# Two first-layer outputs of a fused attention and feed-forward kernel share three cycles of eight stream slots, and their f16 parts move from DVE to POOL

## The chip, the cores and the metric

The kernel runs on one core of one Trainium2 chip. The metric is the device time of one execution in microseconds. Inside the core, PE multiplies matrices, ACT (ScalarE) evaluates exponentials and tanh, DVE (VectorE) does elementwise work, POOL (GpSimd) can do elementwise work on data in SBUF and issues some DMAs, and SP issues most DMAs.

## The reference

The kernel computes a gated sum of an attention with one shared key and value head (32 query heads of width 16) and a feed-forward layer, both of the same `x` (2048 tokens of width 512; the hidden width is 1792):

```
q = (x @ wq) as 32 heads of 16;  k = x @ wk;  v = x @ wv
a = softmax(q k^T / 4) v, heads joined, @ wo
b = silu(x @ w1) @ w2
g = sigmoid(sum(x * gate_w))
out = g * a + (1 - g) * b
```

Everything is f32 at the borders. Inside, the kernel writes an f32 operand as the sum of two f16 parts and multiplies three products of parts (high by high, high by low, low by high).

## The kernel before, in words

A short prologue transposes `x` into f16 parts, makes the keys, values and gate, and the first query blocks. Then `attention` runs one long loop, written out by hand in order: each engine takes its instructions in the order in which this loop issues them.

**Steps and cycles.** The attention is cut into 32 rounds (4 query chunks of 512 tokens, 4 groups of heads, 2 halves) of 16 key tiles, so 512 steps. One pass of the main loop, called a cycle here, issues two steps, so there are 256 cycles. A cycle is spelled as a string of slots:

- S is one score slot: 8 small matmuls (L997) into a PSUM tile of two banks, followed by one exponential on ACT (L1000, 128x1024) into `P`. A cycle has four. There are two such PSUM tiles, so PE can be at most two score slots ahead of ACT.
- F is one slot of the *stream* (L741): 4 matmuls for the lower half of the contraction of a new output and 4 for the upper half of the current one, which use different rows of the array. The stream holds everything that isn't attention: the first feed-forward layer (`ffn_h`), the second (`ffn_o`), the query blocks and the output projection. An output is two turns of 12 slots long (fewer for some): first as the new one, then as the current one. When its second turn is over it is evicted from its PSUM bank; there are two such banks (`pm`), so the next new output starts in the bank that has just been evicted.
- P and N multiply probabilities by values (L1043). The odd step of a cycle always does it with one pass of f32 matmuls (N). The even step does it in one of two ways. *Split*: three passes (PPP) of 16-bit matmuls, by the upper 16 bits of `P`, and by the rest `L`, which DVE must have made with two subtractions of 128x1024 (L1021). *Native*: one more f32 pass (N), with no work on DVE.
- B is the place where a bound for a later round may be made.

**What DVE is given.** `spend`, `put` and `fill` keep an account of DVE's time: each known piece of work has a price, each cycle has a length (3.7 us, 4.1 us after a first-layer output), and small jobs (weight parts, range checks) are filled into what is left. `backlog` is what the account is over.

**First-layer outputs.** 56 of them, in 16 blocks of 4, 4, 4 and 2 per query chunk. `evict` does a tanh on ACT (L789, PSUM to `e`), one combination on DVE (L790, `e` and PSUM to `e`, after which the bank is free), and, up to two cycles later, the two f16 parts on DVE (`split_v`: a cast at L120 and a subtraction at L121, `e` to `H`). The second layer reads `H` a block later. There are two `e` buffers.

**Which even steps are split.** `split_step` says native where the current output is a first-layer one and is in the last half of its turn, or where the cycle is a wide one. 174 even steps are split and 82 are native.

**Wide cycles.** Query blocks are extra work in the stream; each adds 12 to a `debt` (18 at the start). A cycle that follows the eviction of a first-layer output has 12 F slots instead of 6 while the debt is 6 or more (`WIDE`). There are 27 of these.

**The end.** After the last step, the rest of the stream runs as plain 128-row matmuls (L745), with the transposes and division of the last round on DVE ahead of the last output projections.

Of the kernel before, what the change touches and what calls it, by code (L numbers as in the profile page):

```python
# [13 lines left out]
OP = mybir.AluOpType  # L14
# [10 lines left out]


SPLIT, NATIVE = "SFFFSFFFSPPPSBN", "SFFFSFFFSNBSN"
WIDE = {SPLIT: "SFFFFFFSFFFFFFSPPPBSN", NATIVE: "SFFFFFFSFFFFFFSNBSN"}

FIRST = "EEEEEEEEEESEESEEEESEEEESBEEEE"  # L30
AHEAD, EARLY = 2, (4, 5)
# [14 lines left out]
def kernel(  # L46
# [21 lines left out]
    nc = tc.nc  # L68
    _, S, D = x.shape
    F = w1.shape[1]  # L70
    DH = wk.shape[1]
    KD = D // 128
# [17 lines left out]
    xs = consts.tile([128, 2, KD, S], F16)  # L90
# [28 lines left out]
    def split_v(a1, a2, a):  # L119
        nc.vector.tensor_copy(a1, a)  # L120
        nc.vector.tensor_tensor(a2, a, a1, op=OP.subtract)  # L121
# [579 lines left out]
    def attention(ctx, scale_of, t_scale, shifts, split_pieces, chores, q_todo, bounds, early, gates_):  # L701
# [46 lines left out]
        backlog, spent, todo, cycle = [0.0], [0.0], [], [0]  # L748

        def spend(t):  # L750
            spent[0] += t

        def put(t, age, f):

            todo.append((t, cycle[0] + age, f))

        def fill(length):
            room = length - backlog[0] - spent[0]
            cycle[0] += 1
            backlog[0], spent[0] = max(0.0, -room), 0.0  # L760
            if bounds and turn[0] and turn[1] == 6 and not turn[0].hidden and not turn[0].is_q:
                return
            while todo and (todo[0][0] <= room or cycle[0] >= todo[0][1]):
                t, _, f = todo.pop(0)
                f()
                room -= t
            if split_pieces.left() and (room >= 1.3 or split_pieces.count < 5.6 + 0.57 * cycle[0]):
                split_pieces.step()
                room -= 1.3
            elif not split_pieces.left() and chores and (room >= 1.1 or cycle[0] > 200):  # L770
                if chores[0]:
                    chores[0].pop(0)()
                    room -= 1.1
                elif not open_q:
                    chores.pop(1)()
                    room -= 1.1
                    if len(chores) == 1:
                        chores.clear()
            backlog[0] = max(0.0, -room)

        def ffn_h(k, f):
            c, g = blocks[k]
            f0 = (sum(GF[:g]) + f) * 128
            cs = slice(c * 512, c * 512 + 512)

            def evict(ph):

                e = wp.tile([128, 512], F32, name="e", bufs=2)
                nc.scalar.activation(e, ph, AF.Tanh, scale=t_scale)  # L789
                nc.vector.scalar_tensor_tensor(e, e, 1.0, ph, op0=OP.add, op1=OP.mult)  # L790
                H = Hs[k, f] = wp.tile([128, 2, 512], F16, name="H", bufs=2 * NF)
                spend(0.62)
                put(1.0, 2, lambda: split_v(H[:, 0], H[:, 1], e))

            assert split_pieces.ready(w1, g), (k, len(split_pieces.done))
            return Out([(lambda i, b, m, n=32, kt=kt: w1s[b, i, kt, f0 + m:f0 + m + n],
                         lambda j, b, kt=kt: xs[b, j, kt, cs]) for kt in range(KD)], evict, hidden=True)

        def ffn_o(k, t):
            c, g = blocks[k]  # L800
# [57 lines left out]
        urgent = []  # L858

        def outs():  # L860

            for k in range(len(blocks) + 1):
                if k < len(blocks):
                    for f in range(GF[blocks[k][1]]):
                        yield ffn_h(k, f)
                        while urgent:
                            yield urgent.pop(0)()
                else:
                    for _ in range(2):
                        yield urgent.pop(0)() if urgent else None  # L870
                if k:
                    for t in range(4):
                        if queue:
                            debt[0] += 12
                            yield q_block(queue.pop(0))
                        yield ffn_o(k - 1, t)
                        while urgent:
                            yield urgent.pop(0)()
            while True:
                yield urgent.pop(0)() if urgent else None  # L880

        def follow():
            if ahead:
                return ahead.pop()
            o = next(seq)
            if o is not None:
                o.bank = pM.tile([128, 512], F32, name="pm")
            return o

        seq, ahead, ended, debt = outs(), [], [None], [18]  # L890
        drains = [0]
        turn = [None, 0]
        lo, hi_ = slice(0, 64), slice(64, 128)
        plain, ending = [False], [False]
# [1 line left out]
        def stream():  # L896

            cur = None
            while True:
                if plain[0] and cur is None:  # L900
                    o = follow()
                    if o is None:
                        return
                    for n in range(len(o.mm)):
                        o.whole(n, n == 0, n == len(o.mm) - 1)
                    o.evict(o.bank)
                    yield True
                    continue
                new = None if plain[0] else follow()
                n_new = len(new.mm) if new else 0  # L910
                n_cur = len(cur.mm) if cur else 0
                n = -(-max(n_new, n_cur) // 6) * 6


                if cur and drains[0] == cur.count and ending[0]:
                    drain()
                for i in range(n):
                    turn[:] = cur, n - i - 1
                    for m in range(4):
                        if i < n_new:  # L920
                            new.product(i, lo, m, i == 0, False)
                        if i < n_cur:
                            cur.product(i, hi_, m, False, i == n_cur - 1)
                    if i < n - 1:
                        yield False
                if cur:
                    cur.evict(cur.bank)
                    ended[0] = cur
                cur = new
                if cur:  # L930
                    cur.count = drains[0]
                yield True

        def drain():

            nc.tensor.drain()
            drains[0] += 1
# [29 lines left out]
        steps = [(i, kt) for i in range(len(rounds)) for kt in range(NKT)]  # L967
# [37 lines left out]

        def split_step(s):

            return steps[s][1] > 0 and not (turn[0] and turn[0].hidden and (0 < turn[1] <= 6 or wide[0]))

        def low(p, s, j):  # L1010

# [48 lines left out]
                split_pieces.step()  # L1060
                yield

        qtile, wide = {}, [False]
        whole_ = early_products()
        work = stream()
        prefetch(0)
        for s in range(0, len(steps) + 2, 2):
            on = s < len(steps)
            ending[0] = not on
            if on and steps[s][1] == 0:  # L1070
                i = steps[s][0]
                prefetch(i + 1)
                if q_todo and i % 2 == 0:
                    queue.append(q_todo.pop(0))
            p, more = 2 * s, True
            slots, order = SPLIT, [(s - 2, 0), (s - 2, 1), (s - 2, 2), (s - 1, 3)]
            if s - 2 in native:
                slots, order = NATIVE, [(s - 2, 3), (s - 1, 3)]
            if not s and early:
                slots = FIRST  # L1080
            wide[0] = debt[0] >= 6 and ended[0] is not None and ended[0].hidden
            if wide[0]:
                slots = WIDE[slots]
            ended[0], n_f, bounded[0] = None, 0, False
            for a in slots:
                if a == "S" and on:
                    scores(p)
                    p += 1
                elif a == "E":
                    next(whole_, None)  # L1090
                elif a == "F" and more:
                    more = not next(work)
                    n_f += 1
                elif a == "B" and (bound_now() or not s and bounds):
                    bound()
                    bounded[0] = True
                    while lq and lq[0][0] <= p - 3:
                        low(*lq.pop(0))
                elif a in "PN" and s >= 2:
                    pv(*order.pop(0))  # L1100
            debt[0] -= max(n_f - 6, 0)
            if gates_ and s == 4:
                gates_()
                spend(0.6)
            fill(4.95 if n_f > 6 else 4.1 if ended[0] and ended[0].hidden else 3.7)
        plain[0] = True
        while todo:
            todo.pop(0)[2]()
# [6 lines left out]
    over = nc.values_load(flag[0:1, 0:1], min_val=0, max_val=1)  # L1115
# [29 lines left out]
```

## Time and profile before

| | |
|---|---|
| three runs | 1078.17, 1079.02, 1079.59 us; median 1079.02 |
| span of the profiled execution | 1075.3 us, 3.7 us under the median; its time outside the span isn't recorded |
| PE busy | 1057.2 us, 98% |
| ACT busy | 1008.6 us, 94% |
| DVE busy | 789.9 us, 73% |
| POOL busy | 23.4 us, 2% |
| main loop, first to last exponential | 39.3 to 1054.2 us of the span |

The page's first part gives busy time, share of the span and number of instructions for each engine. A group row gives line, engine, operation, what is written from what, count, then busy time, mean duration of one, and the idle time of the engine just before. A row of the table of windows gives the stretch, its length and then the busy time of each engine in it with the number of its instructions. A row of the timeline gives start, length, and how many like instructions were merged. Eight matmuls on different parts of the array run together, so the duration of one (375 ns) is not what a slot costs; what a slot costs is the distance from its start to the next slot's.

### The profile page before, as it was taken

How to read it: one execution, taken by the hardware profiler on the slowest of the kernel's cores; microseconds unless marked ns; L12 is line 12 of the kernel's file. 1: busy time of each engine (PE TensorE's matmuls, PEld its weight loads, DVE VectorE, ACT ScalarE, POOL GpSimd, SP SyncE). 2: the span in 40 equal slices, each digit the busy share in tenths (PEclk: the TensorE clock that was granted, in tenths of full speed). 3: DMA queues.
4: the chain of work that ended last, by engine and by line, in shares of the span. 5: the costliest groups of instructions: out<-in, count | busy, mean ns of one | idle time of the engine just before them, and what ended most of it. 6: DMA issues, size and time to landing. Idle time of an engine off the chain costs nothing.

```text
span 1075.3 us, 65967 instructions
## 1 busy us (share of the span) xinstructions
PE 1057.2 (98%) x31224; PEld 667.5 (62%) x31224; DVE 789.9 (73%) x1082; ACT 1008.6 (94%) x1121; POOL 23.4 (2%) x53
## 2 busy tenths in 40 slices
PE   8999999999999999999999999999999999999996
PEld 5455776766665577677655568677756555555552
DVE  6856986968778786878777697675857767476875
ACT  5799999999999999999999999899989999999992
POOL 2110000000000000000000000000000000000000
PEclk9999999999999999999999999999999999999999
DMA  5311111220001000000000100000000110000001
GB/s 208 115 61 45 49 42 31 61 60 14 11 11 41 32 22 10 17 12 12 22 11 21 37 19 21 22 12 11 20 6 12 31 31 12 11 11 5 11 4 43
DMA packets 20840, 32.95 MB, mean 31 GB/s; under 512 B 5137, under 2 KB 12050, under 8 KB 20562
## 3 DMA queue, kind: packets, MB, share of 16 engines
q1 hardware_dynamic: 17618, 20.46, 5.9%
q0 software_dynamic: 2512, 8.13, 2.6%
q8 instruction: 246, 4.03, 1.5%
q14 instruction: 32, 0.26, 0.1%
q10 hardware_dynamic: 432, 0.07, 0.0%
HBM read 20.12 MB, written 8.52 MB: 27 GB/s over the span
## 4 chain that ended last, share of the span: by engine, by line
PE 89%; DVE 5%; ACT 4%; issue 1%; POOL 0%; POOLq 0%; ACTq 0%
PE pv L1043 35%; PE pm L741 31%; PE S L997 19%; ACT P L1000 4%; DVE L L1021 1%; PE pm L745 1%; PE pt L311 0%; PE pk L126 0%; DVE xs L117 0%; DVE T L943 0%; PE pk L127 0%; PE pk L125 0%; DVE U L944 0%; PE pm L342 0%; DVE T L945 0%
## 5 line engine op out<-in xcount | busy, mean ns | idle before, releaser
L1000 ACT ACTIVATE P<-S 128x1024 f32<-128x1024 f32 x1024 | 963.5, 1051 | 24.6 <-PE S L997 19.4
L997 PE MATMUL S<-qb,KT 50*32 50x512 f16 x8192 | 480.1, 378 | 2.3 <-ACT P L1000 2.2
L1021 DVE TENSOR_TENSOR L<-P 128x1024 f16<-128x1024 f32 x348 | 408.1, 1217 | 8.3 <-ACT P L1000 8.2
L1043 PE MATMUL pv<-P,VF 64*32 64x512 f32 x5408 | 374.8, 589 | 0.0
L997 PEld LDWEIGHTS <-KT 50*32 50x32 f16 x8192 | 188.6, 90 | 193.9 <-issue 126.7
L741 PE MATMUL pm<-w2s,H 64*32 64x512 f16 x5232 | 258.8, 375 | 0.6 <-DVE qx L825 0.2
L741 PE MATMUL pm<-xs,w1s 64*32 64x512 f16 x5376 | 248.5, 375 | 1.1 <-issue 0.6
L741 PEld LDWEIGHTS <-H 64*32 64x32 f16 x5232 | 143.7, 93 | 43.5 <-issue 11.3
L741 PEld LDWEIGHTS <-w1s 64*32 64x32 f16 x5376 | 136.3, 93 | 46.1 <-issue 13.5
L1043 PEld LDWEIGHTS pv<-P,VF 64*32 64x32 f32 x5408 | 125.0, 107 | 30.3 <-issue 8.1
L790 DVE SCALAR_TENSOR_TENSOR e<-e,pm 128x512 f32<-128x512 f32 x56 | 38.5, 687 | 140.3 <-ACT e L789 139.4
L1043 PE MATMUL pv<-P,VH 64*32 64x512 bf16 x1392 | 81.9, 389 | 0.0
L1043 PE MATMUL pv<-L,VH 64*32 64x512 f16 x1392 | 81.4, 374 | 0.0
L1043 PE MATMUL pv<-P,VL 64*32 64x512 bf16 x1392 | 81.4, 385 | 0.0
L741 PE MATMUL pm<-xs,wqs 64*32 64x512 f16 x1152 | 81.1, 375 | 0.0
L1043 PEld LDWEIGHTS <-VH 64*32 64x32 f16 x2784 | 60.7, 92 | 20.4 <-issue 3.8
L741 PE MATMUL pm<-wo_s,O 64*32 64x512 f16 x1440 | 63.3, 375 | 0.0
L943 DVE STREAM_TRANSPOSE T<-pv 128x512 f32<-128x512 f32 x32 | 23.0, 717 | 48.0 <-PE pv L1043 40.4
L722 DVE SCALAR_TENSOR_TENSOR acc<-pm,g,acc 128x512 f32<-128x512 f32 x48 | 35.8, 745 | 26.4 <-PE pm L741 24.6
L741 PEld LDWEIGHTS <-wqs 64*32 64x32 f16 x1152 | 43.6, 93 | 10.1 <-issue 2.8
L121 DVE TENSOR_TENSOR H<-e,H 128x512 f16<-128x512 f32 x56 | 38.8, 693 | 1.9
L789 ACT ACTIVATE e<-pm 128x512 f32<-128x512 f32 x56 | 34.5, 616 | 5.7 <-PE pm L741 5.7
(155 smaller groups left out, 478.9 us busy)
## 6 DMA issues: line engine op xcount, KB each, us to landing
qb<-qd SPq DMA_DIRECT2D x192, 32.0 KB
raw<-in_B_w_dram POOLq DMA_DIRECT2D x23, 256.0 KB, 2.9
xn<-in_A_x_dram SPq DMA_DIRECT2D x8, 512.0 KB
out_dram<-acc SPq DMA_DIRECT2D x16, 256.0 KB
qd<-qx SPq DMA_DIRECT2D x12, 256.0 KB
raw<-in_A_wo_dram POOLq DMA_DIRECT2D x4, 256.0 KB, 3.6
qb<-sh SPq DMA_DIRECT2D x62, 2.0 KB
raw<-in_B_w_dram SPq DMA_DIRECT2D x3, 256.0 KB
```

The source lines that it names most:

```text
L121: nc.vector.tensor_tensor(a2, a, a1, op=OP.subtract)
L722: nc.vector.scalar_tensor_tensor(a, po, gate[:, n:n + 1], a, op0=OP.mult, op1=OP.add)
L741: nc.tensor.matmul(self.bank[32 * m:32 * m + 32], l(i, rows, 32 * m), r(j, rows), start=first, stop=last)
L745: nc.tensor.matmul(self.bank, l(i, slice(0, 128), 0, 128), r(j, slice(0, 128)), start=first, stop=last)
L789: nc.scalar.activation(e, ph, AF.Tanh, scale=t_scale)
L790: nc.vector.scalar_tensor_tensor(e, e, 1.0, ph, op0=OP.add, op1=OP.mult)
L943: nc.vector.transpose(T, pv[0])
L997: nc.tensor.matmul(sc[32 * m:32 * m + 32, f], KT[b:b + 50, k0:k0 + 32], qtile[i][b:b + 50, j], start=True, stop=True)
L1000: nc.scalar.activation(P[:, 2 * j:2 * j + 2], sc, AF.Exp, scale=scale_of(c, o))
L1021: nc.vector.tensor_tensor(lows[s][:, q], P[:, q], upper(P)[:, q], op=OP.subtract)
L1043: nc.tensor.matmul(pvs[i][h][32 * j:32 * j + 32], a[r], b[r, j], start=first, stop=last)
```

## The change

1. `WIDE` goes; `PAIR` comes. Three cycles in a row get 8 F slots each. They start when the current output is the first of a pair (`hidden` is now 1 for an even and 2 for an odd first-layer output) with its whole second turn of 12 slots ahead, and the debt is 6 or more. So the 24 slots of the three cycles are just the second turns of two first-layer outputs. The first is evicted in the middle cycle after its first four slots, the second in the last cycle after all eight. An output projection no longer comes between the two of a pair.
2. The f16 parts of a first-layer output are made on POOL, right after L790, and no longer on DVE a cycle or two later.
3. An even step is split whenever DVE's account is less than 1 us over; where the first-layer outputs stand no longer matters.
4. The account's price of L790 is 0.69 instead of 0.62; the account's length of a cycle is 4.1 in the three cycles, and 3.7 or 4.1 elsewhere as before (4.95 goes).
5. At the end the stream no longer stops at the first empty place. The debt of a second pass (code that runs only for inputs out of range, not here) starts at 0.

```
-WIDE = {SPLIT: "SFFFFFFSFFFFFFSPPPBSN", NATIVE: "SFFFFFFSFFFFFFSNBSN"}
+PAIR = ({SPLIT: "SFFFFSFFFFSPPPSBN", NATIVE: "SFFFFSFFFFSNBSN"},
+        {SPLIT: "SFFFFSPPPSNSFFFF", NATIVE: "SFFFFSNSNSFFFF"},
+        {SPLIT: "SFFFFSFFFFSPPPSBN", NATIVE: "SFFFFSFFFFSNBSN"})
...
-                spend(0.62)
-                put(1.0, 2, lambda: split_v(H[:, 0], H[:, 1], e))
+                spend(0.69)
+                nc.gpsimd.tensor_copy(H[:, 0], e)
+                nc.gpsimd.tensor_tensor(H[:, 1], e, H[:, 0], op=OP.subtract)
...
-                         lambda j, b, kt=kt: xs[b, j, kt, cs]) for kt in range(KD)], evict, hidden=True)
+                         lambda j, b, kt=kt: xs[b, j, kt, cs]) for kt in range(KD)], evict, hidden=1 + f % 2)
...
-                        while urgent:
+                        while urgent and f % 2:
...
-                cur = new
+                cur = turn[0] = new
+                turn[1] = 12
...
-            return steps[s][1] > 0 and not (turn[0] and turn[0].hidden and (0 < turn[1] <= 6 or wide[0]))
+            return steps[s][1] > 0 and backlog[0] < 1.0
...
-            wide[0] = debt[0] >= 6 and ended[0] is not None and ended[0].hidden
-            if wide[0]:
-                slots = WIDE[slots]
+            if not pair[0] and debt[0] >= 6 and s and turn[0] and turn[0].hidden == 1 and turn[1] == 12:
+                pair[0] = 3
+            if pair[0]:
+                slots = PAIR[3 - pair[0]][slots]
...
-                elif a == "F" and more:
-                    more = not next(work)
+                elif a == "F":
+                    next(work)
...
-            fill(4.95 if n_f > 6 else 4.1 if ended[0] and ended[0].hidden else 3.7)
+            fill(4.1 if pair[0] or ended[0] and ended[0].hidden else 3.7)
+            pair[0] = max(pair[0] - 1, 0)
```

More of the change, by code (lines that the diff above doesn't have):

```diff
@@ L878, in outs @@
                             yield urgent.pop(0)()
+            over[0] = True
             while True:
@@ L888, in follow @@
             return o
-        seq, ahead, ended, debt = outs(), [], [None], [18]
-        drains = [0]
+        seq, ahead, ended, debt = outs(), [], [None], [18 if q_todo else 0]
+        drains, over = [0], [False]
         turn = [None, 0]
@@ L902, in stream @@
                     if o is None:
-                        return
+                        if over[0]:
+                            return
+                        continue
                     for n in range(len(o.mm)):
@@ L1061, in early_products @@
                 yield
-        qtile, wide = {}, [False]
+        qtile, pair = {}, [0]
         whole_ = early_products()
@@ L1074, in attention @@
                     queue.append(q_todo.pop(0))
-            p, more = 2 * s, True
+            p = 2 * s
             slots, order = SPLIT, [(s - 2, 0), (s - 2, 1), (s - 2, 2), (s - 1, 3)]
```

## The prediction

> **What bounds the kernel now.** I read the page's busy shares first, then the chain that ended last, then the groups, then a table of windows cut at the first score slot of chosen cycles.
>
> ```profile
> PE 1057.2 (98%) x31224; PEld 667.5 (62%) x31224; DVE 789.9 (73%) x1082; ACT 1008.6 (94%) x1121; POOL 23.4 (2%) x53
> ...
> PE 89%; DVE 5%; ACT 4%; issue 1%; POOL 0%; POOLq 0%; ACTq 0%
> ```
>
> PE is busy throughout and carries 89% of the chain. ACT at 94% looks like a second bound, so its own pace has to be known:
>
> ```profile
> 49.14 2.85 ACT L1000 ACTIVATE P<-S 128x1024 f32<-128x1024 f32 x3
> ...
> 319.34 0.68 ACT L789 ACTIVATE e<-pm 128x512 f32<-128x512 f32 x1
> 319.82 5.70 ACT L1000 ACTIVATE P<-S 128x1024 f32<-128x1024 f32 x6
> ...
> L1000 ACT ACTIVATE P<-S 128x1024 f32<-128x1024 f32 x1024 | 963.5, 1051 | 24.6 <-PE S L997 19.4
> ```
>
> Unhindered, three exponentials of 1.05 us take 2.85, so one follows another after (2.85 - 1.05)/2 = 0.90 us; a tanh takes 0.48 (319.34 to 319.82). A cycle costs ACT 4 x 0.90 = 3.60, and 4.08 with a tanh. What it costs PE is in the windows, in this order: split with 6 F slots, native with 6, split with 12 (wide), native with 12, and two neighbours: a native cycle with a first-layer eviction and the split one behind it.
>
> ```profile
> 343.52:347.22 3.70, 3.70 (x128) 2.06 (x120) 3.58 (x4) 3.70 (x5) 0.00 (x0) 1.00 0.21 75
> 335.92:339.82 3.90, 3.90 (x121) 1.91 (x113) 3.50 (x7) 3.90 (x5) 0.00 (x0) 1.00 0.20 72
> 58.97:63.98 5.01, 5.01 (x177) 2.93 (x175) 4.09 (x6) 4.51 (x6) 0.00 (x0) 1.00 0.01 3
> 63.98:69.17 5.19, 5.19 (x169) 2.82 (x161) 2.90 (x7) 4.56 (x6) 0.55 (x1) 1.00 0.15 54
> 316.99:320.99 4.00, 4.00 (x121) 2.01 (x105) 1.33 (x3) 4.00 (x6) 0.00 (x0) 1.00 0.02 4
> 320.99:324.81 3.82, 3.82 (x128) 1.99 (x127) 3.79 (x5) 3.82 (x5) 0.00 (x0) 1.00 0.02 4
> ```
>
> So PE is the bound in almost every cycle: 3.70 against ACT's 3.60. An F slot costs (5.01 - 3.70)/6 = 0.218. A native even step costs 0.20 more than a split one (3.90 against 3.70; 0.18 in the wide pair). Only a first-layer output in a 6-slot cycle makes ACT the longer one: 4.08 of tanh and exponentials against 3.90, and the two neighbours take 4.00 + 3.82 where PE alone needs 3.90 + 3.70.
>
> **The change, part by part.** Counts are from the instruction order of the two programs.
>
> *More split steps.* The subtractions into `L` go from 348 to 430, so 41 even steps turn from native to split: 41 x 0.19 (between 0.18 and 0.20) = -7.8 us on PE. The chance that this doesn't happen is nil, since the program shows it; only whether PE gets the time back is open.
>
> *First-layer outputs out of the 6-slot cycles.* Before, 35 are evicted in 6-slot cycles and 21 in wide ones; after, 2 and 54. Each of the 33 cost 4.00 + 3.82 - 3.90 - 3.70 = 0.22, so -7.3 us. This takes the one pair of rows for all 33; the bounds are 0 and -7.3.
>
> *Three cycles of 8 for one of 12.* There are 27 either way with 6 extra slots each, so PE pays nothing new. An 8-slot split cycle costs PE 3.70 + 2 x 0.218 = 4.14, ACT with its tanh 4.08. The margin is 0.06, so I cost it at nothing; without that margin each of 54 evictions would pay up to the 0.22 above.
>
> *The end.* The stream runs 5 slots more (1698 against 1693), since it no longer stops at the first empty place: +1.1 us. One more second-layer output of 6 plain matmuls comes after the last projections' first group.
>
> ```profile
> 1060.41 4.47 PE L745 MATMUL pm<-wo_s,O 128*128 128x512 f16 x12 [2.21 <-DVE O L120]
> 1064.90 4.04 PE L745 MATMUL pm<-w2s,H 128*128 128x512 f16 x18
> ```
>
> The 18 run at (4.04 - 0.38)/17 = 0.215 each, so the 12 need 2.6 and wait some 1.8 for their two banks. The 6 cost 1.3 and stand where that wait is: nothing, bounds -0.5 and +1.3. The removed drain is one instruction at the end: nothing.
>
> *DVE.* It loses the two parts and gains the subtractions.
>
> ```profile
> L1021 DVE TENSOR_TENSOR L<-P 128x1024 f16<-128x1024 f32 x348 | 408.1, 1217 | 8.3 <-ACT P L1000 8.2
> L790 DVE SCALAR_TENSOR_TENSOR e<-e,pm 128x512 f32<-128x512 f32 x56 | 38.5, 687 | 140.3 <-ACT e L789 139.4
> L121 DVE TENSOR_TENSOR H<-e,H 128x512 f16<-128x512 f32 x56 | 38.8, 693 | 1.9
> L120 DVE CAST H<-e 128x512 f16<-128x512 f32 x56 | 23.7, 423 | 0.6
> ...
> sum 1014.90, PE 1010.98 PEld 643.19 DVE 754.60 ACT 985.73 POOL 16.50; mean PE 126.37 PEld 80.40 DVE 94.32 ACT 123.22 POOL 2.06
> ```
>
> Off: 38.8 + 23.7 = 62.5. On: 82 x 408.1/348 = 96. In the main loop (the sum row) DVE goes from 755 to 788 of about 1000 us, so on average there is room. What counts is lateness in single places. L790 waits on DVE's queue for the tanh (139.4 us in all), and now two subtractions of 1.17 stand behind it in the same cycle, where before such cycles were native. That a late subtraction holds PE is in the trace:
>
> ```profile
> 256.87 2.35 DVE L1021 TENSOR_TENSOR L<-P 128x1024 f16<-128x1024 f32 x2
> 258.63 0.47 PE L1043 MATMUL pv<-P,VL 64*32 64x512 bf16 x8
> 258.85 0.82 PE L1043 MATMUL pv<-L,VH 64*32 64x512 f16 x8
> ```
>
> DVE is done with `L` at 259.22 and the eight products take 0.82 instead of 0.47: PE lost 0.35.
>
> In the last cycle of a triple the eighth F slot ends after 2 S and 8 F, 10 x 0.218 = 2.2; tanh and L790 (0.69) follow and end near 3.7; the subtractions end near 3.7 + 2.35 = 6.05. PE needs them in the next cycle after 3 S, 6 F and two P: 4.14 + 11 x 0.218 = 6.5, or 7.0 if that cycle has 8. The slack is 0.5 (15 triples) or 0.9 (12 that are followed by another). In the middle cycle the first output is done after 1 S and 4 F, L790 near 2.75, `L` near 5.1, needed at 4.14 + 13 x 0.218 = 7.0; that has room. Its bank is wanted after 4 S, 4 F, PPP and N: 12 x 0.218 less one S already run, so near 3.2; slack 0.5 as well.
>
> *POOL.* 112 new instructions, none like them in the trace. The nearest:
>
> ```profile
> L209 POOL MEMSET VH<- 128x512 f16 x1 | 0.5, 524 | 0.0
> ...
> L207 POOL MEMSET qb<- 128x1024 f16 x2 | 1.8, 951 | 0.0
> ...
> L303 POOL COPY wkv<-wkr 128x64 f32<-128x64 f32 x1 | 0.2, 236 | 0.1
> ...
> L178 POOL DMA_DIRECT2D raw<-in_B_w_dram x27 | 14.7, 544 | 186.0 <-DVE w1s L196 99.8 <-DVE w2s L196 64.0 <-DVE wqs L196 14.2
> ```
>
> The cast lies between 0.52 and 0.95, the subtraction reads two operands and so between 1.05 and 1.9; together 1.6 to 2.9. I take 1.6, the row of equal size on the same engine. Evictions are at least 4.1 us apart and `H` is read a block later, so POOL's own time is hidden; it would cost only if it passed 4 us an output. The weight loads on POOL's queue (L178) now stand behind it; three buffers and one load a cycle at most leave them cycles of room: nothing. The loads wait for DVE work that stands ahead of L790 on DVE, so they don't hold POOL's parts either.
>
> Whether a running POOL instruction holds up a DVE subtraction isn't in any row: in the main loop POOL does no elementwise work today. Bounds: it doesn't (0), or each subtraction that meets one waits it out. In the last cycle that is 1.6 less 0.5 of slack, 1.1 x 27 = 30 us; by 2.9 it is 65. I take +5. The two subtractions run with no gap (2.35 for two of 1.217), and POOL can only begin when L790 is through, when DVE already starts the first; a POOL instruction would have to slip in between. That is nearer 0 than 30, but DVE's own lateness, like the 0.35 above, is in it too.
>
> The Trainium skill's page "SBUF — State Buffer", section "Who interferes with whom", speaks against the change: a DVE instruction with two SBUF inputs and a GpSimd instruction that reads SBUF share one read interface, and whichever comes second is blocked until the first is through. `L` is made of two views of `P`, both in SBUF. By that rule the term is nearer the 30, and the sum would be 1095; without it, 1065 to 1070. No run here shows it.
>
> **Sum.** -7.8 - 7.3 + 1.1 + 5 = -9.0. Against the median of 1079.0: 1070.0. The profiled span is 3.7 under the median; I carry the difference from one to the other unchanged.
>
> **Rivals.**
>
> *POOL holds the subtractions (slower).* Place: last cycle of each triple, and the first F slot after an eviction, where L790 has become late. Price 1.1 us a triple, 30 in all: 1079.0 - 14.0 + 30 = 1095. It decides from 14.0/27 = 0.52 us a triple. For it: slack of 0.5 in three places at once, and DVE's queue is in order. Against: L790 itself reads PSUM and one tile, and 0.5 to 0.9 of slack absorbs a cast.
>
> *ACT stays the bound of first-layer cycles (no change).* The 0.06 of margin doesn't hold: the tanh sits behind an exponential, DVE's L790 is late, and 54 evictions pay 0.22 each, +11.9 in place of the +5: 1079.0 - 7.8 - 7.3 + 1.1 + 11.9 = 1076.9, and with some lateness 1077 to 1081. For it: 4.08 against 4.14 is tight. Against: wide cycles, which have more slots for one tanh, run at PE's 5.01 and 5.19.
>
> *DVE's relief tells more.* No new lateness, and some of today's goes, since 1.1 us of work per output leaves DVE: 1079.0 - 14.0 = 1065, down to 1060.
>
> **How the numbers follow.** About 0.2% (2.2 us) is what a measurement here tells from no change. Forecast, 1065 to 1076.8: 0.50. More gain, under 1065: 0.10. No change, 1076.9 to 1081.2: 0.13. Slower: 0.27, spread from 1081 to 1095 and beyond. So faster 0.60, same 0.13, slower 0.27. The forecast's own range is 1065 to 1077. The range for 8 in 10 is 1063 to 1088: it leaves out some 0.05 below and 0.13 above.
>
> **What the profile after would show.** Right: 430 subtractions at L1028; windows of 8-slot split cycles near 4.14; the score slots of cycles with a tanh as close as PE allows; POOL near 56 x 1.6 = 90 us more busy; DVE near 820. Wrong: subtractions with a mean well above 1217 ns; products of `L` that take much more than 0.50 at the end of a triple; F slots after an eviction that wait for L792 on DVE. The forecast falls if these add more than half a microsecond a triple.

## The result and the profile after

The change makes the kernel slower: 1089.22 us (1088.42 to 1089.63) against 1079.3 us for the kernel before, a ratio of 1.0094 with a 95% interval of 1.008 to 1.0108. Forecast was 1070.0. The profiled execution of after has a span of 1087.2 us, 11.9 more than before's 1075.3.

The page of after, its busy shares and its chain:

```profile
PE 1054.2 (97%) x31510; PEld 676.0 (62%) x31510; DVE 858.9 (79%) x1052; ACT 1015.1 (93%) x1121; POOL 220.0 (20%) x165
...
PE 82%; DVE 11%; ACT 4%; issue 2%; DMA 0%; ACTq 0%; POOL 0%
```

PE is busy 3.0 us less than before in a span that is 11.9 longer: the new time is waiting. DVE's share of the chain went from 5% to 11%. The groups and the waits of after say more (group rows as before; a row of waits gives who waits, for whom, the total, how often, and the longest):

```profile
L1028 DVE TENSOR_TENSOR L<-P 128x1024 f16<-128x1024 f32 x430 | 531.4, 1282 | 8.9 <-ACT P L1007 8.8
L795 POOL CAST H<-e 128x512 f16<-128x512 f32 x56 | 88.4, 1579 | 628.2 <-DVE e L792 628.2
L796 POOL TENSOR_TENSOR H<-e,H 128x512 f16<-128x512 f32 x56 | 107.5, 1919 | 4.5
L792 DVE SCALAR_TENSOR_TENSOR e<-e,pm 128x512 f32<-128x512 f32 x56 | 38.4, 685 | 50.7 <-ACT e L791 50.7
...
PE pm L743 <- DVE e L792: 6.9, 5, 1.4
```

Three things are new. A subtraction for `L` takes 1282 ns on average instead of 1217. POOL's two instructions take 1.58 and 1.92 us. And five times PE's F slots wait for L792 on DVE, 6.9 us in all; before has no such row.

To see where the span went, I cut both traces at the first score slot of every cycle and subtracted from each cycle what its slots alone cost on PE: 3.70 for a split and 3.89 for a native cycle of 6 F slots, and 0.217 for each F slot more. The very first cycle has slots of its own and is counted as cost in full (5.01 in both). What is left over is called excess here.

| us | before | after | difference |
|---|---|---|---|
| start of the first cycle | 38.8 | 39.2 | +0.4 |
| what the slots cost (255 cycles) | 995.5 | 987.7 | -7.8 |
| excess | 15.5 | 32.5 | +17.0 |
| from the last cycle to the end | 25.5 | 27.8 | +2.3 |
| span | 1075.3 | 1087.2 | +11.9 |

So the gain of 7.8 us that 41 more split steps were to bring is there in full. It is given back in excess, and most of that sits in six cycles. The table of windows of after shows all six native middle cycles (`SFFFFSNSNSFFFF`; the first triple does not begin with a round, the other five do). Its second row is the first cycle of the triple whose middle cycle is the third row, and its last row is one split cycle. The busy times are those of PE, PEld, DVE, ACT and POOL; the last three columns are the granted clock, the busy share of the DMA engines and GB/s.

```profile
158.92:163.25 4.33, 4.33 (x131) 2.68 (x123) 3.16 (x6) 4.33 (x6) 2.47 (x3) 1.00 0.23 64
360.35:364.48 4.13, 4.13 (x144) 2.25 (x142) 0.70 (x1) 4.01 (x5) 0.00 (x0) 1.00 0.20 45
364.48:370.76 6.28, 4.91 (x136) 2.27 (x128) 5.77 (x10) 4.96 (x6) 0.85 (x1) 1.00 0.04 10
430.26:436.69 6.43, 5.06 (x137) 2.79 (x129) 5.78 (x10) 5.13 (x6) 0.85 (x1) 1.00 0.04 9
496.44:502.88 6.44, 5.07 (x136) 2.72 (x128) 5.77 (x10) 5.12 (x6) 0.84 (x1) 1.00 0.01 3
561.09:567.37 6.28, 4.91 (x136) 2.44 (x128) 5.77 (x10) 4.98 (x6) 0.85 (x1) 1.00 0.05 11
942.05:948.43 6.38, 5.01 (x137) 2.55 (x128) 5.78 (x10) 5.05 (x6) 0.85 (x1) 1.00 0.01 3
796.36:804.53 8.17, 5.29 (x128) 3.35 (x120) 3.75 (x4) 4.44 (x5) 0.00 (x0) 0.79 0.02 2
```

The five take 6.28 to 6.44 instead of 4.33: 10.2 us together. In each DVE runs ten instructions instead of six and is busy nearly throughout. The timeline of the first of them shows what these are (start, length, engine, line, operation; in brackets the idle time and who ended it):

```profile
364.78 0.72 DVE L950 STREAM_TRANSPOSE T<-pv 128x512 f32<-128x512 f32 x1 [3.73 <-PE pv L1050]
365.42 0.67 DVE L951 STREAM_TRANSPOSE U<-pv 128x512 f32<-128x512 f32 x1
365.88 0.60 ACT L791 ACTIVATE e<-pm 128x512 f32<-128x512 f32 x1
366.13 0.44 DVE L952 TENSOR_TENSOR T<-T,U 128x272 f32<-128x272 f32 x1
...
366.60 0.25 DVE L954 RECIPROCAL rr<-T 128x16 f32<-128x16 f32 x1
...
366.89 0.42 DVE L957 TENSOR_TENSOR C<-T,rr 128x256 f32<-128x256 f32 x1
...
367.35 0.71 DVE L961 STREAM_TRANSPOSE T<-C 128x512 f32<-128x512 f32 x1
...
368.10 0.43 DVE L122 CAST O<-T 128x512 f16<-128x512 f32 x1
...
368.56 0.69 DVE L123 TENSOR_TENSOR O<-T,O 128x512 f16<-128x512 f32 x1
369.17 0.68 DVE L792 SCALAR_TENSOR_TENSOR e<-e,pm 128x512 f32<-128x512 f32 x1
369.77 2.77 DVE L1028 TENSOR_TENSOR L<-P 128x1024 f16<-128x1024 f32 x2
369.90 1.06 PE L743 MATMUL pm<-xs,w1s 64*32 64x512 f16 x32 [1.37 <-DVE e L792]
370.76 0.41 PE L1004 MATMUL S<-qb,KT 50*32 50x512 f16 x8
```

The last product of a round's probabilities comes at the end of a triple's first cycle. DVE, which sat idle for 3.73 us until then, now has the whole end of the round ahead of it: two transposes out of PSUM, the sum, the reciprocal, the product, a third transpose and the parts of `O`, 4.4 us in one row. The tanh of the triple's first output is done at 366.48, but L792, which stands behind all that in DVE's queue, starts only at 369.17. The middle cycle's second four F slots need the bank that L792 frees. PE stands for 1.37 us after the last matmul of the score slot before, and the F slots start 5.42 us into the cycle; in the first experiment below the same cycle reaches them at 3.46. So the whole 2.0 us of such a cycle are the wait for the bank.

Why these middle cycles are native: `split_step` never splits a round's first step, and the step's products come one cycle after its scores. A triple that begins with a round therefore has a native middle cycle. The native form goes with the round's end; it is not what costs.

The long split cycle (796.36) has another cause. Inside it, from 798.30 to 801.70, PE runs next to nothing and its idle time ends with no release:

```profile
798.30:801.70 3.40, 0.52 (x19) 0.03 (x3) 2.05 (x2) 0.57 (x1) 0.00 (x0) 0.89 0.00 0
```
```profile
801.68 0.63 PE L1050 MATMUL pv<-P,VH 64*32 64x512 bf16 x4 [2.88 <-issue]
```

The DMA view for 794 to 804 shows two packets of instructions (16 KB each) in 3.6% of 16 engines' 10 us, that is 2.9 us a packet, among 128 packets of 4 bytes, the range check's maxima, which SP sends to DRAM at 793.68:

```profile
q8 instruction: 2, 0.03, 3.6%
q1 hardware_dynamic: 144, 0.00, 0.8%
...
md<-raw SPq DMA_DIRECT2D x1, 0.5 KB
```

The kernel before sends the same packets and loses 1.0 + 0.35 us beside them; after loses 4.47. So of the 17.0 us of excess, 10.2 are the five middle cycles, 3.1 this stop, and 3.7 is the rest. Half of this rest is one split 6-slot cycle that begins at 113.60 and takes 5.54 us. There a query block's eviction stands on DVE behind a round's third transpose and two weight parts, and PE waits for its bank:

```profile
115.57 0.37 PE L743 MATMUL pm<-xs,wqs 64*32 64x512 f16 x1 [1.56 <-DVE qx L828]
```

### The profile page after: what moved, and what is told of

Same layout as the page of the kernel before. It is cut to its first block, busy times and chain, and to the rows that moved or that the text cites. A ratio compares the mean times of both kernels' runs of the same rounds, so it can differ in the third digit from the quotient of the medians.

```text
span 1087.2 us, 66647 instructions
## 1 busy us (share of the span) xinstructions
PE 1054.2 (97%) x31510; PEld 676.0 (62%) x31510; DVE 858.9 (79%) x1052; ACT 1015.1 (93%) x1121; POOL 220.0 (20%) x165
## 3 DMA queue, kind: packets, MB, share of 16 engines
q8 instruction: 248, 4.06, 1.6%
## 4 chain that ended last, share of the span: by engine, by line
PE 82%; DVE 11%; ACT 4%; issue 2%; DMA 0%; ACTq 0%; POOL 0%
PE pv L1050 32%; PE pm L743 29%; PE S L1004 18%; ACT P L1007 4%; DVE L L1028 3%; PE pm L747 1%; DVE T L950 1%; DVE U L951 1%; DVE e L792 1%; DVE T L952 1%; DVE T L961 1%; DVE C L957 1%; DVE acc L724 1%; DVE mxs L137 0%; ACT e L791 0%
## 5 line engine op out<-in xcount | busy, mean ns | idle before, releaser
L1028 DVE TENSOR_TENSOR L<-P 128x1024 f16<-128x1024 f32 x430 | 531.4, 1282 | 8.9 <-ACT P L1007 8.8
L1004 PE MATMUL S<-qb,KT 50*32 50x512 f16 x8192 | 499.4, 378 | 1.1 <-ACT P L1007 0.9
L1050 PE MATMUL pv<-P,VF 64*32 64x512 f32 x4752 | 338.1, 590 | 0.0
L795 POOL CAST H<-e 128x512 f16<-128x512 f32 x56 | 88.4, 1579 | 628.2 <-DVE e L792 628.2
L796 POOL TENSOR_TENSOR H<-e,H 128x512 f16<-128x512 f32 x56 | 107.5, 1919 | 4.5
L1050 PE MATMUL pv<-P,VH 64*32 64x512 bf16 x1720 | 105.1, 390 | 2.9 <-issue 2.9
L1050 PE MATMUL pv<-L,VH 64*32 64x512 f16 x1720 | 106.0, 375 | 0.7 <-DVE raw L644 0.3
L1050 PE MATMUL pv<-P,VL 64*32 64x512 bf16 x1720 | 104.6, 387 | 0.0
L1050 PEld LDWEIGHTS <-VH 64*32 64x32 f16 x3440 | 80.0, 93 | 33.0 <-issue 10.2
L792 DVE SCALAR_TENSOR_TENSOR e<-e,pm 128x512 f32<-128x512 f32 x56 | 38.4, 685 | 50.7 <-ACT e L791 50.7
L1050 PEld LDWEIGHTS <-VL 64*32 64x32 f16 x1720 | 38.9, 94 | 11.3
```

The source lines that it names most:

```text
L795: nc.gpsimd.tensor_copy(H[:, 0], e)
L796: nc.gpsimd.tensor_tensor(H[:, 1], e, H[:, 0], op=OP.subtract)
L1004: nc.tensor.matmul(sc[32 * m:32 * m + 32, f], KT[b:b + 50, k0:k0 + 32], qtile[i][b:b + 50, j], start=True, stop=True)
L1028: nc.vector.tensor_tensor(lows[s][:, q], P[:, q], upper(P)[:, q], op=OP.subtract)
L1050: nc.tensor.matmul(pvs[i][h][32 * j:32 * j + 32], a[r], b[r, j], start=first, stop=last)
```

## The experiments

The theories: the round's end in front of L792 (first); PE out of instructions beside the small packets (second); POOL's reads against DVE's subtractions, the prediction's own suspect (third).

### The round's end, moved

Where a triple begins with a round, all of the round's end but the two transposes is issued at the end of the middle cycle, after L792:

```
-                norm_a(pvs.pop(i), rb, state)
-                spend(2.4)
-                if rb == 1:
-                    put(0.65, 3, ...)
+                rest = norm_a(pvs.pop(i), rb, state)   # the two transposes
+                spend(1.4)
+                def then():                            # sum, reciprocal, product; then put(...) as before
+                    rest()
+                    spend(1.0)
+                    ...
+                if pair[0] == 3:
+                    late.append(then)
+                else:
+                    then()
...
+            if late and pair[0] == 2:
+                late.pop()()
             fill(...)
```

> The changed kernel, but where a triple of 8-slot cycles begins in the first cycle of a round, only the two transposes of the round's end stay in that cycle; the sum, reciprocal, product and what follows on DVE are issued at the end of the middle cycle, behind the eviction's L792. Bank theory (five native middle cycles take 6.3 to 6.4 us instead of 4.33, because L792 stands behind the round's end on DVE and the next F slot needs its bank): these five go to about 4.5, 5 x 2.0 = 10 us less, so about 1079. Port theory (POOL's parts hold DVE up, and that is the loss): POOL's work is the same, so 1089 within 2.

It took 1077.3 us, a ratio to before of 0.9985 (0.9974 to 0.9996): 11.9 us less than after. The middle cycles that begin with a round, in its windows:

```profile
364.74:369.06 4.32, 4.32 (x128) 2.33 (x120) 4.03 (x6) 4.16 (x6) 1.09 (x1) 1.00 0.02 6
428.97:433.45 4.48, 4.48 (x130) 2.77 (x121) 4.03 (x5) 4.32 (x6) 0.95 (x1) 1.00 0.03 8
493.53:497.99 4.46, 4.46 (x130) 2.83 (x121) 4.03 (x5) 4.32 (x6) 0.95 (x1) 1.00 0.04 9
557.32:561.64 4.32, 4.32 (x128) 2.31 (x120) 3.57 (x5) 4.18 (x6) 1.51 (x1) 1.00 0.04 11
```

The 6.28 to 6.44 became 4.32 to 4.48, with PE busy all through. In the first of them, L792 and the F slots behind it (which follow 3.46 us after the cycle's start) now stand so:

```profile
367.24 0.67 DVE L792 SCALAR_TENSOR_TENSOR e<-e,pm 128x512 f32<-128x512 f32 x1
...
368.20 0.38 PE L743 MATMUL pm<-xs,w1s 64*32 64x512 f16 x1
```

These are four cycles, not five: in this kernel the last of the five triples begins two cycles behind the round, at 936.62, since the account placed other work anew. Excess fell by 10.5, from 32.5 to 22.0. In the four cycles it fell by 7.9, of which the cycle behind each pays 0.26 back (4.41 instead of 4.15). The fifth triple's 2.0 went because that triple moved, and 2.7 are a shorter stop beside the small packets (1.74 instead of 4.47). The end got 1.7 shorter too, for a reason that was not looked into. The first theory holds where the chain was moved. That the time fell by more than the whole slowdown (11.9 against 9.9 us between the medians) is partly the work of these other shifts.

### The maxima in four rows

The 128 maxima are transposed once more and leave as 4 rows of 128 bytes, in after, in the kernel of the first experiment, and in before:

```
-            mt, mr = raw_[0][:, 0:32], raw_[0][:, 32:33]
+            mt, mr, mw = raw_[0][:, 0:32], raw_[0][:, 32:33], raw_[0][:, 32:64]
...
-            nc.sync.dma_start(md.rearrange("(p o) -> p o", o=1), mr)
+            nc.vector.transpose(mt, mw)
+            nc.sync.dma_start(md.rearrange("(p o) -> p o", o=32), mt[0:97:32])
```

> The changed kernel, but the 128 maxima of the range check leave as 4 rows of 128 bytes (one more 32x32 transpose on DVE) instead of 128 packets of 4 bytes. Fetch theory (beside the two others: PE's instruction fetch stands behind these packets, a 16 KB packet takes 3.5 us instead of 0.9, and the split cycle at 796 us takes 8.17 instead of 3.70): that cycle goes to 3.7 to 4, 3 to 4.5 us less, about 1085. If the stop has another cause: 1089 within 1, and the cycle near 8.

> The changed kernel with both cures: the rest of the round's end behind the middle cycle's eviction where a triple begins with a round, and the 128 maxima as 4 rows. By the bank and fetch theories the two add: 1089.2 - 10.2 - 4.5 = 1074.5, between 1073.5 and 1076.5, ratio to the kernel before 0.995 to 0.997; no 8-slot cycle over 5 us and none near 780 us of the span that stops. If the two overlap, 1077 as with the first alone.

> The kernel before with the 128 maxima as 4 rows. Fetch theory: its wide native cycle at 790 us goes from 6.22 to 5.19 and the next from 4.24 to 3.89, 1.4 us less, ratio 0.9987, about what a measurement tells. If the stop there has another cause, both cycles stay.

After with rows: 1084.24 us, 1.0048 (1.0031 to 1.0064). Both cures: 1075.6, 0.9967 (0.9956 to 0.9978). Before with rows: 1076.77, 0.9976 (0.9966 to 0.9986). The row is worth 5.0 us in after, 1.7 behind the first cure and 2.6 in before, where the trace of before had led to expect 1.4. In after with rows the same split cycle is an ordinary one, and four packets of instructions between 790 and 804 take 2.0% of 16 engines' 14 us, 1.1 us each:

```profile
796.29:800.01 3.72, 3.72 (x128) 2.96 (x120) 3.50 (x4) 3.72 (x5) 0.00 (x0) 1.00 0.02 5
```
```profile
q8 instruction: 4, 0.07, 2.0%
```

The second theory holds in that the stop goes with the small packets. That PE lacked instructions meanwhile is inferred from the time of the packets and from idle time that no release ends; no row shows it directly. It is no part of what the change does: before has the same defect and gains from the same cure. The same packets cost 1.4, 1.7, 3.2 and 4.5 us in four kernels; presumably this depends on where PE's next block of instructions falls, which was not tested. With both cures the changed kernel is only 1.2 us better than before with the row, and the intervals overlap.

### POOL's share

Three runs. POOL clears `H` with two memsets that read nothing (this leaves out the parts of the first layer, so the feed-forward result is not computed); before with the parts on POOL and nothing else; after with the parts on DVE:

```
-                nc.gpsimd.tensor_copy(H[:, 0], e)
-                nc.gpsimd.tensor_tensor(H[:, 1], e, H[:, 0], op=OP.subtract)
+                nc.gpsimd.memset(H[:, 0], 0.0)
+                nc.gpsimd.memset(H[:, 1], 0.0)
```
```
 before:
-                put(1.0, 2, lambda: split_v(H[:, 0], H[:, 1], e))
+                nc.gpsimd.tensor_copy(H[:, 0], e)
+                nc.gpsimd.tensor_tensor(H[:, 1], e, H[:, 0], op=OP.subtract)
```

The third, in after, is the reverse of the second, with `spend(0.62)` again.

> The changed kernel, but POOL sets both f16 parts of a first-layer output to zero (two memsets of 128x512 that read nothing) instead of a cast and a subtraction; the feed-forward part of the output is left out by that. Order of everything else is the same. Port theory: the subtractions into L fall from 1282 to 1217 ns, and the time falls by 10 or more, to 1079 or below. Bank theory: the 1282 may fall, but the five native middle cycles stay at 6.3; only the waits of PE for L (4.6 us against 2.0 before the change) can go, so 1085 to 1088.

> The kernel before with one part of the change alone: the f16 parts are made on POOL right after L790 instead of on DVE. Slots, wide cycles and the choice of native steps stay (348 subtractions). Port theory: slower by 10 or more, 1089 or above. Bank theory: there is no triple, so no more than 3 us either way, 1076 to 1082; POOL's two instructions take 1.5 to 1.9 us each as they do in the changed kernel where they meet subtractions, less where the cycle is native.

> The changed kernel with the f16 parts back on DVE, as the kernel before makes them (on the account at 1.0, up to two cycles late); 424 subtractions into L instead of 430. If POOL's share of the loss is what the memsets gave back (4 us, some 1 of it another fetch), DVE's own 62 us of parts come in its place: subtractions at 1217 ns, the native middle cycles still 6 us or more, time 1084 to 1092. If POOL were the main loss, 1080 or less.

Memsets: 1084.92 us, 1.0058 (1.0041 to 1.0075), 4.3 less than after; 1.2 of that is a shorter stop beside the small packets (3.23 for 4.47). Before with POOL: 1081.5, 1.0022 (1.0011 to 1.0034), 2.0 more than before; 0.8 of that is a longer stop (1.75 + 0.43 instead of 1.02 + 0.35). After with the parts on DVE: 1084.31, 1.0038 (1.0024 to 1.0052), 4.9 less than after. This last has one round's end less in front of a middle cycle (four, not five; 2.0 us). On the other side, PE waits 2.10 us once for a query block's eviction that stands behind a range check of 2.28 us on DVE. DVE's order differs throughout, so POOL's part of the 4.9 is not separated. The groups, first with memsets, then with the parts in before:

```profile
L1028 DVE TENSOR_TENSOR L<-P 128x1024 f16<-128x1024 f32 x430 | 503.1, 1217 | 9.1 <-ACT P L1007 9.1
...
L795 POOL MEMSET H<- 128x512 f16 x56 | 29.5, 526 | 702.6 <-PE pm L743 697.6 <-remote 3.2 <-PE S L1004 1.8
```
```profile
L1022 DVE TENSOR_TENSOR L<-P 128x1024 f16<-128x1024 f32 x348 | 425.4, 1267 | 11.4 <-ACT P L1001 11.4
...
L794 POOL TENSOR_TENSOR H<-e,H 128x512 f16<-128x512 f32 x56 | 93.4, 1668 | 4.6
L793 POOL CAST H<-e 128x512 f16<-128x512 f32 x56 | 63.2, 1129 | 665.7 <-DVE e L790 659.6 <-DVE raw L642 6.1
```

With POOL reading nothing, the subtraction is back at 1217 ns; with POOL reading, in either kernel, it is not. Other work of DVE is held up as well. In before with POOL, a cast of `O` that meets POOL's subtraction (627.18 to 629.21) takes 1.39 us instead of 0.42. The query block's eviction behind it comes later, and PE waits:

```profile
628.10 1.39 DVE L120 CAST O<-T 128x512 f16<-128x512 f32 x1
...
631.59 0.37 PE L741 MATMUL pm<-xs,wqs 64*32 64x512 f16 x1 [0.83 <-DVE qx L826]
```

This cycle takes 4.81 us instead of the 3.70 that it takes in before. So the two do hold each other up. In after it costs about 3 us, by the memsets, the one pair with the same order; in before, 1.1 us in this one cycle. The native middle cycles stayed at 6.3 to 6.45 with memsets: they are not POOL's.

### The round's end later at every round, in both kernels

With the row in place, the rest of the round's end goes one cycle later at every round, not only where a triple starts. In before, the two steps behind it keep their cycle. A third run is the changed kernel of this kind with the parts on DVE.

```
-                if pair[0] == 3:
-                    late.append(then)
+                if on:
+                    late.append((s, then))
...
-            if late and pair[0] == 2:
-                late.pop()()
+            while late and late[0][0] < s - 1:
+                late.pop(0)[1]()
```

> As the kernel with both cures, but the rest of the round's end is issued one cycle later at every round, not only where a triple begins with it (43 native steps instead of 41). If evictions in other cycles lose to the round's end too (89 and 105: 4.77 instead of 3.89), 1 to 3 us less again: 1072 to 1075. If what is moved only makes later subtractions late: 1075 or more.

> The kernel before the change with the row of maxima, and with the rest of a round's end one cycle later at every round (the two steps behind it keep the cycle in which they stood). It has no triples. If the later round's end helps because it stands ahead of first-layer evictions whose bank PE wants soon, it does little here, where wide cycles evict once in 6 or 14 slots: 1076 to 1077, as with the row alone (1076.8), and the 3.4 us by which e8_late_everywhere is better are the change's own, once its two costs are cured. If the later round's end helps any cycle that starts behind a round (second-layer and projection evictions too), it gives here the 2.2 us that it gave between e6_late_and_row and e8_late_everywhere: 1074 to 1075, and the change itself is then worth about 1 us.

> The kernel of e8_late_everywhere (row of maxima, the round's end one cycle later at every round) with the first layer's two f16 parts made on DVE again, as before the change; the schedule's account is charged for them. If POOL's reading beside DVE costs what the earlier pairs showed (4.3 us with two memsets in their place, 4.9 us with the parts on DVE, both against the changed kernel), the time falls from 1073.4 to 1068.5-1071.5 and the mean of the subtraction that makes a step's lower part falls to 1215-1220 ns. If those gains were those of the round's end alone (DVE's queue being later by POOL's share just there), nothing is left to win once the round's end is out of the way, and the time stays within 2 us of 1073.4 or rises, because DVE has 56 x 1.3 us more work.

| | median us | ratio to before (95%) | slots | excess | end |
|---|---|---|---|---|---|
| before, row, late | 1073.71 | 0.9948 (0.9929 to 0.9966) | 995.5 | 11.9 | 25.6 |
| after, row, late | 1073.41 | 0.9943 (0.9926 to 0.9959) | 988.1 | 16.5 | 28.7 |
| after, row, late, parts on DVE | 1067.15 | 0.9889 (0.9871 to 0.9907) | 988.7 | 8.8 | 27.7 |

The late round's end is no special cure of triples: it gives 2.2 us in after and 3.1 in before. Between the kernels with all cures, before and after, nothing is left of the change while the parts are on POOL (0.3 us, within the intervals); with the parts on DVE it is worth 6.6 us, and the time lies below the 1068.5 to 1071.5 that was expected. That kernel is the fastest, 1.1% under before. Its groups show the subtraction at 1217 ns again, and a whole triple with a split middle cycle goes at PE's pace:

```profile
L1032 DVE TENSOR_TENSOR L<-P 128x1024 f16<-128x1024 f32 x420 | 493.1, 1217 | 9.6 <-ACT P L1011 9.3
```
```profile
426.34:430.48 4.14, 4.14 (x145) 3.69 (x137) 4.07 (x7) 4.02 (x5) 0.00 (x0) 1.00 0.02 4
430.48:434.74 4.26, 4.26 (x145) 3.23 (x137) 4.22 (x6) 4.23 (x6) 0.00 (x0) 1.00 0.02 4
434.74:438.87 4.13, 4.13 (x144) 2.20 (x136) 3.38 (x6) 4.11 (x6) 0.00 (x0) 1.00 0.01 4
```

The 6.3 us between the last two kernels are not all reading conflicts. In the kernel with the parts on POOL, two split middle cycles take 5.75 (this one, from its windows, is the same cycle as the second row above):

```profile
433.27:439.02 5.75, 4.77 (x145) 2.94 (x137) 5.68 (x8) 5.03 (x6) 0.85 (x1) 1.00 0.01 3
```

There the third transpose and the parts of `O` stand ahead of the eviction once more (transpose at 435.62, eviction at 437.43), while with the parts on DVE the account placed the parts of `O` behind the eviction. POOL has a hand in it all the same: in both cycles DVE's chain comes a microsecond later than it would, because the sum at its head takes 1.4 us beside POOL's subtraction instead of 0.44.

```profile
431.26 1.42 DVE L955 TENSOR_TENSOR T<-T,U 128x272 f32<-128x272 f32 x1
```

These two cycles are about 3.0 of the 6.3. How much of the 6.3 is the conflict itself and how much the account's other order was not separated.

## Why the prediction was wrong

**41 native steps turn split, -7.8: right.** The slots' cost fell by just that, 995.5 to 987.7.

**First-layer outputs out of the 6-slot cycles, -7.3: somewhat too large.** It took one pair of rows (4.00 + 3.82) for all 33. Over all 35 such cycles of before the mean is 3.98, 0.09 above a plain native one, so 3.1 together. The overlong neighbour was typical, but only where the next cycle has 6 slots: 22 such neighbours pay 2.8 together (the split ones take 3.81 to 3.83), while the other 13 are wide cycles and pay 0.1 in all. So some 5.9 us were there in before, within the bounds given. How much of them came back was not separated; between the last table's first and third kernels the excess falls by 3.1 in all.

**Three cycles of 8 for one of 12, 0: right where nothing stands in front.** The split third cycle of a triple, the one with the tanh, takes 4.15 on average in after and in the fastest kernel; 4.14 was reckoned. The rival by which ACT stays the bound fails on this.

**The end, +1.1: measured +2.3, from another place.** The five slots hold no work: the stream makes 13152 small products instead of 13200. The first of the last projections starts 10.6 us after the last cycle begins in both kernels, so PE's longer wait there, 3.90 us instead of 2.21, is not new time either:

```profile
1070.04 1.33 PE L747 MATMUL pm<-wo_s,O 128*128 128x512 f16 x3 [3.90 <-DVE O L122]
```

What is longer comes behind it. The projections and the six plain products take 6.39 us (1070.04 to 1076.43), where the projections alone took 4.49. The six cost 1.9, above the upper bound of 1.3; they do not stand under the wait for the banks, as was assumed.

**DVE and POOL, +5: POOL's share about 3, the working wrong.** That 5 lies near it is luck. POOL's parts were costed at 1.6 us, bounds 1.6 to 2.9. Alone they need 0.61 + 1.17 (the shortest ones in the trace); met by DVE they take 1.54 + 2.03, above the upper bound. Their means in the profile sum to 3.5. DVE lost (1282 - 1217) x 430 = 28 us in its subtractions, near the 30 that the other end of the range gave, and 34 in all (858.9 us busy, against 824.9 beside POOL's memsets). But the kernel lost only about 3 us by it; slack must have taken the rest. My reason for the low value, that POOL would have to slip between two subtractions, is refuted by the timeline: the cast starts at 369.91, 0.14 after the first subtraction, and the pair takes 2.77 instead of 2.35.

The Trainium skill, page "SBUF — State Buffer", section "Who interferes with whom", says that a DVE instruction with two SBUF inputs and a GpSimd instruction that reads SBUF exclude each other, and one that only writes does not. The traces agree in both halves: 1282 ns beside POOL's cast and subtraction, 1217 beside its memsets. What it does not decide is the time of the kernel.

**The step that failed: the middle cycle's bank.** The prediction gave L792 "near 2.75" and the bank's need "near 3.2; slack 0.5 as well". It reckoned this for a split middle cycle and took DVE to be free when the tanh ends. In the five native middle cycles L792 ends 5.37 us into the cycle (369.85 - 364.48 in the first), since a round's end of 4.4 us stands ahead of it on DVE. The need was not the error: the sum as written gives 2.4, not 3.2 (3.05 with N at the 0.87 that the 6-slot cycle leaves for it), and in the native form the first experiment shows it at 3.46, later than reckoned. The prediction listed what of the change was new on DVE, but not what was already in its queue at that place: before's waits show the chain's place, DVE waiting for a round's last product 26 times, and I did not follow it into the new triples.

```profile
DVE T L943 <- PE pv L1043: 40.4, 26, 3.1
```

The price is 10.2 us, twice what was set aside for all lateness and by far the largest of the terms that the sum lacked. The first experiment undoes it in the four cycles that it reaches (8.1 us of excess before, 0.3 after).

**Not in the sum: PE's instructions.** The small packets cost before 1.4 us and after 4.5. Nothing in before's page pointed at it but two long cycles.

By the measured terms: -7.8 + 10.2 + 3.1 + 2.3 + 0.4 and 3.7 for the rest (new lateness with POOL's share, less the evictions' gain) = +11.9. The slower rival was the right sign by another mechanism, and its 1.1 us a triple with 27 triples became 2.0 in five of them.

## What to carry to other kernels

When an eviction that frees a bank is moved, list everything that its engine already has in its queue at that place, in each phase of the loop and not only in the usual cycle: a chain that runs once in sixteen steps costs nothing until somebody waits behind it. Work moved to an idle engine is not free when it holds up the busy engine's own reads: with the two other costs cured, undoing that one part turned a change worth nothing into one worth 6.6 us, part of which is the other order of DVE's work.

## What was not expected of the hardware

- A cast of 128x512 on POOL took 0.61 us alone and 1.54 us beside DVE's subtractions; a two-input subtraction 1.17 and 2.03. DVE's pair took 2.77 instead of 2.35. DVE's cast of 128x512 and its sum of 128x272 took 1.39 and 1.42 us beside POOL's subtraction, 0.42 and 0.44 elsewhere.
- Beside 128 packets of 4 bytes to DRAM, 16 KB packets of instructions took 2.9 us instead of 1.1, and PE lost up to 4.5 us. Four packets of 128 bytes did not. The Trainium skill, page "Runtime: NRT & Kernel Launch", section "Instruction fetch mechanics", has each engine fetch its next block of 16 KiB while it works on the one before, the cost of passing from one to the next being mostly hidden. The trace agrees with the size (248 packets, 4.06 MB); if the stop is a fetch, here is a case where it was not hidden.
